# Attention with a relative position bias, then a bilinear feed-forward layer: the band factor made by one-hot products on TensorE, and the first four feed-forward steps interleaved with the last attention pair of batch 0

## The chip, the cores and the metric

The kernel runs on one core of a Trainium2 chip. The metric is the time of one execution on the device in microseconds (us); lower is better. The engines are called as in the profile: PE (TensorE matmuls, with PEld for its weight loads), DVE (VectorE), ACT (ScalarE), POOL (GpSimd) and SP (SyncE, which here only issues transfers).

## What is computed

Inputs are q, k, v of 8 batches, 8 heads, 576 positions and 64 channels, a bias table of 32 buckets by 8 heads, and three weight matrices. The attention output, its heads side by side, is the x of the feed-forward layer.

```python
scores = scale * np.matmul(q, k.transpose(0, 1, 3, 2))      # scale = 1/8
n = np.abs(pos[:, None] - pos[None, :])
bucket = ...            # n itself below 16, then logarithmic, 31 at most
scores = scores + bias_table[bucket].transpose(2, 0, 1)[None]
attn = np.exp(scores - max) / sum
x = matmul(attn, v)     # (8*576, 512), heads side by side
out = ((x @ w_a) * (x @ w_b)) @ w_out        # d_ff = 1536
```

From a distance of 129 on, all positions are in the last bucket. So the kernel multiplies exp(score) by exp(bias - last bias) only in a band around the diagonal; the factor of the last bucket cancels in the softmax.

## The kernel before

**Pairs.** Attention goes by 32 pairs of heads: pair p is batch p // 4, heads 2hp and 2hp + 1 with hp = p % 4. `emit_scores(p, i)` makes the transposed scores of key tile i (128 keys) for both heads into one slot of a ring of two PSUM slots (tag "st"), and ACT takes their exp (L269). `emit_scores_rest` does the last 64 keys and queries (L277, L285, exps L280 and L287). `emit_mult` multiplies the band by the band factor `E_sb` (L303; L298 for the last key tile in batch 0; from pair 4 on the copy `Et_sb`). `emit_av` multiplies by v with a column of ones (L320 for the last 64 keys of both heads, L323 for the others), DVE divides (L331, L333) into `xg`, and `emit_x` transposes that into `xn` (for batch 0 on PE with a copy on DVE, L348 and L349; later by a DMA).

**Band factor.** `emit_table` loads the table (L169), its last row (L170) and a one-hot matrix (L172), subtracts on DVE, takes the exp on ACT, multiplies by the one-hot matrix on PE (L179) to get, for each head, a row of 512 factors by distance, and stores it 32 times over to DRAM (L182). Twelve loads on SP (L188) read it back with a step of 511, one column further for each partition, as `E_sb` (128 x 8 heads x 384), first for heads 0 and 1, then 2 and 3, then 4 to 7; four more (L195) fill `Et_sb`.

**Loads.** All other inputs come by POOL's queue in the program's order: q and k of batch 0 in three parts, v, the first halves of w_a and w_b (`load_w_in(0)`), half of batch 1's q and k, the second halves, the rest of batch 1, w_out. PE transposes q and k for pairs 0 to 9 (`emit_transposes_first`, `emit_transposes`), and ACT or DVE copies them out of PSUM.

**Order.** The order on each engine is that of the program (a manual schedule). In pairs 0 to 3 no feed-forward work can run, as x of batch 0 isn't there yet; matmuls on zeros (`emit_warm`, L403) stand between pair 0's scores. Then come `emit_x(2)`, av of pair 3, `emit_x(3)`, and `QUANTA_FIRST` = 4 feed-forward quanta. A quantum is four matmuls of 512 columns: w_a or w_b (L361, L369) for one slice of 128 of the 1536 channels, with a copy on ACT (L365) or a product on DVE (L372) after it; or a third of an output tile (L378). From pair 4 on each pair has nine steps, and quanta are put between them so that the 36 of the first 512 rows are done by step 47, and one a step from then on.

**Banks.** Four more PSUM banks are used in turn: m0 and m1 for "av" (av, x, table and warm-up), m2 and m3 for "ffn" (quanta, and q/k transposes of batch 0). After pair 3, "av" has m0 alone and "ffn" the other three.

Of the kernel before, what the change touches and what calls it, by code (L numbers as in the profile page):

```python
# [13 lines left out]
def kernel(  # L14
# [11 lines left out]
    nc = tc.nc  # L26
# [42 lines left out]
    assert (bucket_of(np.arange(129, S)) == NB - 1).all()  # L69
    yy = np.arange(512)  # L70
    oh_np = np.zeros((NB, 512), dtype=np.float32)
    oh_np[bucket_of(np.abs(255 - yy)), yy] = 1.0
    oh_handle = nc.inline_tensor(oh_np.astype(ml_dtypes.bfloat16), name="oh_const")
# [83 lines left out]
    oh_sb = const.tile([NB, 512], BF16, name="oh_sb")  # L157
    bt_sb = const.tile([NB, H], FP32, name="bt_sb")
    bl_sb = const.tile([NB, H], FP32, name="bl_sb")
    bd_sb = const.tile([NB, H], FP32, name="bd_sb")  # L160
    eb_sb = const.tile([NB, H, 16], BF16, name="eb_sb")
    tab_sb = const.tile([128, 512], BF16, name="tab_sb")

    tab_dram = nc.dram_tensor("tab_scratch", [H, 32, 512], BF16, kind="Internal")
# [3 lines left out]
    def emit_table():  # L168
        nc.sync.dma_start(out=bt_sb[:, :], in_=bias_table)  # L169
        nc.sync.dma_start(out=bl_sb[:, :],  # L170
                          in_=bias_table[NB - 1:NB, :].to_broadcast([NB, H]))
        nc.sync.dma_start(out=oh_sb[:, :], in_=oh_handle.ap())  # L172
        nc.vector.tensor_tensor(out=bd_sb[:, :], in0=bt_sb[:, :], in1=bl_sb[:, :], op=SUB)

        nc.scalar.activation(
            out=eb_sb[:, :, :],
            in_=bd_sb[:, :].rearrange("b (h a) -> b h a", a=1).to_broadcast([NB, H, 16]), func=ACTF.Exp)
        tp = bank("av", [128, 512], FP32, "tab_ps")
        nc.tensor.matmul(out=tp[:, :], lhsT=eb_sb[:, :, :].rearrange("b h a -> b (h a)"), rhs=oh_sb[:, :],  # L179
                         start=True, stop=True)  # L180
        nc.vector.tensor_copy(out=tab_sb[:, :], in_=tp[:, :])
        nc.sync.dma_start(  # L182
            out=tab_dram.ap().rearrange("h (r a) c -> (h r) a c", a=2),
            in_=tab_sb[:, :].rearrange("p (a c) -> p a c", a=1).to_broadcast([128, 2, 512]))

        for h0, h1 in ((0, 2), (2, 4), (4, H)):
            for r0 in range(0, 128, 32):
# [199 lines left out]
    def all_quanta():  # L387
        for c in range(NCH):
            yield from ffn_quanta(c)

    quanta = all_quanta()


# [48 lines left out]
    for p in range(4):  # L442
# [26 lines left out]
        if p == 0:  # L469
            emit_warm(2)  # L470
# [119 lines left out]
```

## Time and profile before

| | |
|---|---|
| three runs | 418.82, 419.52, 420.39 us (median 419.52) |
| profiled execution | 419.12 us |
| its span | 417.4 us, granted clock 0.998 |
| PE busy | 402.5 us (96%) |
| DVE, ACT, POOL busy | 233.9, 231.2, 79.0 us |
| bytes moved | 47.71 MB, 11.75 MB of them in the first 70 us |
| first quantum on PE | 35.09 us |
| first scores of pair 4 | 39.22 us |

The span goes from the first instruction to the last; the execution has 1.7 us more around it. A matmul's busy time includes its way through the array, and successive matmuls overlap, so PE's share is an upper bound. In a group of instructions or a timeline, a row gives the engine, the line, the operation, what is written from what, and in brackets how long the engine had been idle and what released it.

### The profile page before, as it was taken

The page shows a single profiled execution, that of the slowest core. Times are in us where ns is not written, and L with a number is a line of the kernel's source. Part 1 is how long each engine was busy: PE and PEld are TensorE (multiplying, and loading weights), DVE is VectorE, ACT ScalarE, POOL GpSimd, SP SyncE. Part 2 cuts the span into 40 slices and gives each one's busy share as a digit, 9 for nine tenths or more (in the row PEclk, how much of TensorE's full clock was granted, in tenths as well). Part 3 has the DMA queues.
Part 4 walks back from the last instruction along what each step waited for, and adds up shares of the span by engine and source line. Part 5 has one row for each costly group of instructions (what it writes and reads, how often), then busy time and mean ns, then how long its engine had stood idle before and what let it go on. Part 6 is the DMA issues. An engine that isn't in the chain of part 4 may idle for free.

```text
span 417.4 us, 8452 instructions
## 1 busy us (share of the span) xinstructions
PE 402.5 (96%) x3346; PEld 206.4 (49%) x3404; DVE 233.9 (56%) x568; ACT 231.2 (55%) x313; POOL 79.0 (19%) x136
## 2 busy tenths in 40 slices
PE   8789899999999999999999999999999999999996
PEld 2455355555455455454555555454554554444442
DVE  3486666676555755575556656665556553332331
ACT  4984788566755665476646674567556631321320
POOL 8744641113111311103011311130000000000000
PEclk9999999999999999999999999999999999999999
DMA  9999999699759686978697977983342012002002
GB/s 111 183 209 206 166 189 105 135 208 158 107 94 207 114 100 104 213 102 112 102 178 136 134 103 151 177 127 52 71 121 45 17 40 93 2 0 101 2 0 101
DMA packets 111176, 47.71 MB, mean 114 GB/s; under 512 B 85120, under 2 KB 106528, under 8 KB 111136
## 3 DMA queue, kind: packets, MB, share of 16 engines
q0 software_dynamic: 54304, 18.88, 42.2%
q1 hardware_dynamic: 56832, 28.29, 28.0%
q8 instruction: 26, 0.43, 0.4%
q14 instruction: 14, 0.11, 0.1%
HBM read 38.77 MB, written 16.19 MB: 132 GB/s over the span
## 4 chain that ended last, share of the span: by engine, by line
PE 85%; DMA 8%; POOL 3%; issue 2%; DVE 1%; ACT 1%; POOLq 0%; DVEq 0%
PE po L378 23%; PE pb L369 21%; PE pa L361 21%; PE av L323 8%; PE st L267 7%; DMA wb<-in_moe_w_b_dram 6%; PE av L320 2%; DMA vb<-in_v_dram 2%; PE st L285 2%; PE st L277 1%; POOL vb L129 1%; POOL kl L108 0%; PE tr L219 0%; POOL ql L108 0%; ACT at L269 0%
## 5 line engine op out<-in xcount | busy, mean ns | idle before, releaser
L269 ACT ACTIVATE at<-st 128x1024 bf16<-128x1024 f32 x128 | 124.0, 1022 | 52.1 <-PE st L267 51.2
L372 DVE TENSOR_TENSOR g<-pb,ha 128x512 bf16<-128x512 f32 x108 | 74.6, 691 | 77.0 <-PE pb L369 54.0
L365 ACT ACTIVATE ha<-pa 128x512 f32<-128x512 f32 x108 | 64.7, 599 | 92.2 <-PE pa L361 91.0
L369 PE MATMUL pb<-xn,wb 128*128 128x512 bf16 x407 | 109.0, 379 | 1.5
L361 PE MATMUL pa<-xn,wa 128*128 128x512 bf16 x417 | 108.8, 379 | 0.5
L378 PE MATMUL po<-wo,g 128*128 128x512 bf16 x415 | 99.7, 379 | 0.8
L303 DVE TENSOR_TENSOR at<-at,E 128x768 bf16<-128x768 bf16 (+2 forms) x128 | 61.5, 501 | 7.9 <-DMA E<-tab_scratch 4.1
L323 PE MATMUL av<-vb,at 128*128 128x65 bf16 x1280 | 64.7, 194 | 0.3 <-DVE at L303 0.2
L378 PEld LDWEIGHTS <-g 128*128 128x128 bf16 x432 | 39.6, 98 | 49.1 <-issue 7.9
L323 PEld LDWEIGHTS <-at 128*128 128x128 bf16 x1280 | 55.4, 98 | 16.5 <-issue 1.2
L369 PEld LDWEIGHTS <-wb 128*128 128x128 bf16 x432 | 38.7, 97 | 46.4 <-issue 8.0
L361 PEld LDWEIGHTS <-wa 128*128 128x128 bf16 x432 | 38.4, 97 | 43.2 <-issue 7.0
L382 DVE COPY ob<-po 128x512 f32<-128x512 f32 x36 | 24.9, 691 | 53.9 <-PE po L378 53.9
L267 PE MATMUL st<-qkT 64*128 64x512 bf16 x256 | 40.8, 385 | 2.6 <-ACT at L280 0.9
L320 PE MATMUL av<-vb,at 128*128 128x130 bf16 x160 | 35.4, 221 | 2.5 <-DVE xn L349 1.2
L496 POOL COPY pace<-at 1x1 bf16<-1x1 bf16 x22 | 4.2, 193 | 173.0 <-DVE at L303 172.9
L333 DVE TENSOR_TENSOR xg<-av,rc 128x384 bf16<-128x384 f32 x64 | 31.4, 491 | 2.2
L129 POOL DMA_DIRECT2D vb<-in_v_dram x36 | 30.7, 864 | 7.9 <-PE pb L369 2.2
L280 ACT ACTIVATE at<-st 128x512 bf16<-128x512 f32 x32 | 19.1, 597 | 23.0 <-PE st L277 23.0
L331 DVE RECIPROCAL rc<-av 128x6 f32<-128x6 f32 x64 | 11.8, 184 | 27.6 <-PE av L323 27.6
L320 PEld LDWEIGHTS <-at 128*128 128x128 bf16 x160 | 15.6, 98 | 17.1 <-issue 1.6
L287 ACT ACTIVATE at<-st 128x576 bf16<-128x576 f32 x32 | 20.7, 646 | 0.0
(51 smaller groups left out, 177.8 us busy)
## 6 DMA issues: line engine op xcount, KB each, us to landing
out_dram<-ob SPq DMA_DIRECT2D x36, 256.0 KB, 2.3
qk_scratch<-qkn SPq DMA_DIRECT2D x22, 288.0 KB, 4.5
ql<-in_q_dram POOLq DMA_DIRECT2D x15, 288.0 KB, 5.7
kl<-in_k_dram POOLq DMA_DIRECT2D x15, 288.0 KB, 6.9
vb<-in_v_dram POOLq DMA_DIRECT2D x28, 128.0 KB, 6.7
wa<-in_moe_w_a_dram POOLq DMA_DIRECT2D x4, 384.0 KB, 13.9
wb<-in_moe_w_b_dram POOLq DMA_DIRECT2D x4, 384.0 KB, 13.6
wo<-in_moe_w_out_dram POOLq DMA_DIRECT2D x4, 384.0 KB, 7.9
```

Source lines behind the costliest of these rows:

```text
L129: nc.gpsimd.dma_start(out=vb2[b % 2][:, h0:h1, i, 0:Dh], in_=v[b, h0:h1, 128 * i:128 * i + 128, :].transpose([1, 0, 2]))
L267: nc.tensor.matmul(out=st[:, hh, :], lhsT=kT[r, 128 * i:128 * i + 128], rhs=qT[r, 0:512], start=True, stop=True)
L269: nc.scalar.activation(out=at[:, 2 * i:2 * i + 2, 0:512], in_=st[:, :, :], func=ACTF.Exp, scale=scale)
L303: nc.vector.tensor_tensor(out=at[:, sl, q0:q0 + w], in0=at[:, sl, q0:q0 + w], in1=e, op=MULT)
L320: nc.tensor.matmul(out=pav[:, j, :, :], lhsT=at[:, 8, 128 * jq:128 * jq + 128], rhs=vb[:, 2 * hp:2 * hp + 2, 4, :], start=True, stop=False)
L323: nc.tensor.matmul(out=pav[:, j, hh, :], lhsT=at[:, 2 * i + hh, 128 * jq:128 * jq + 128], rhs=vb[:, 2 * hp + hh, i, :], start=False, stop= ...
L333: nc.vector.tensor_tensor(out=xo.rearrange("p j (h d) -> p j h d", h=2), in0=pav[:, :, :, 0:Dh], in1=rc[:, 0:n, :, :].to_broadcast([128, n ...
L361: nc.tensor.matmul(out=ps[:, :], lhsT=wa_sb[:, mc, 128 * df:128 * df + 128], rhs=xn[:, mc, 512 * c:512 * c + 512], start=(mc == 0), stop=( ...
L365: nc.scalar.activation(out=ha[:, :], in_=ps[:, :], func=ACTF.Copy)
L369: nc.tensor.matmul(out=ps[:, :], lhsT=wb_sb[:, mc, 128 * df:128 * df + 128], rhs=xn[:, mc, 512 * c:512 * c + 512], start=(mc == 0), stop=( ...
L372: nc.vector.tensor_tensor(out=g[:, df, :], in0=ps[:, :], in1=ha[:, :], op=MULT)
L378: nc.tensor.matmul(out=ps[:, :], lhsT=g[:, df, 128 * tt:128 * tt + 128], rhs=wo_sb[:, df, :], start=(df == 0), stop=(df == NDF - 1))
```

## The change

The band factor is no longer read from DRAM. Four one-hot matrices, one above the other (32 rows each, shifted by one position each), and a mask are one constant of 128 x 544. The table stands four times in 128 partitions. A product of 128 one-hot columns with the 128 x 32 right side (four blocks on the diagonal, one for each shift) gives four columns of the band for 8 heads; 16 such products fill a bank, and DVE copies it to 64 columns of `E_sb`, heads first. Six bands (`emit_band(0)` to `emit_band(5)`) stand in pair 0 in the places of warm-up matmuls (eleven go, the first six and the last two stay). `Et_sb` is copied from `E_sb` on POOL. The DVE memsets of `set_k` and `set_at` move ahead of the table. The loads from `load_w_in(1)` on stand behind pair 0's `emit_scores_rest`, with the copy of `Et_sb` among them.

The first four quanta become `EarlyQuanta`: two of their accumulators in one slot of the "st" ring, two in the "ffn" banks; each `part(mc)` runs the four matmuls of one head pair's rows of x, and parts stand before and after pair 3's av and `emit_x(3)`. `emit_x(2)` copies on ACT. Two more quanta come before pair 4, `QUANTA_FIRST` is 6.

```diff
     yy = np.arange(512)
-    oh_np = np.zeros((NB, 512), dtype=np.float32)
-    oh_np[bucket_of(np.abs(255 - yy)), yy] = 1.0
-    oh_handle = nc.inline_tensor(oh_np.astype(ml_dtypes.bfloat16), name="oh_const")
+    oh_np = np.zeros((4, NB, 544), dtype=np.float32)
+    for g in range(4):
+        oh_np[g, bucket_of(np.abs(252 - yy + g)), yy] = 1.0
+        oh_np[g, :, 512 + 8 * g:520 + 8 * g] = 1.0
+    oh_handle = nc.inline_tensor(oh_np.reshape(4 * NB, 544).astype(ml_dtypes.bfloat16), name="oh_const")
     ident = const.tile([128, 128], BF16, name="ident")
...
-    oh_sb = const.tile([NB, 512], BF16, name="oh_sb")
-    bt_sb = const.tile([NB, H], FP32, name="bt_sb")
-    bl_sb = const.tile([NB, H], FP32, name="bl_sb")
-    bd_sb = const.tile([NB, H], FP32, name="bd_sb")
-    eb_sb = const.tile([NB, H, 16], BF16, name="eb_sb")
-    tab_sb = const.tile([128, 512], BF16, name="tab_sb")
-    tab_dram = nc.dram_tensor("tab_scratch", [H, 32, 512], BF16, kind="Internal")
+    oh_sb = const.tile([128, 544], BF16, name="oh_sb")
+    bt_sb = const.tile([128, H], FP32, name="bt_sb")
+    bl_sb = const.tile([128, H], FP32, name="bl_sb")
+    eb_sb = const.tile([128, H], FP32, name="eb_sb")
+    ebd_sb = const.tile([128, 4, H], BF16, name="ebd_sb")
     E_sb = wpool.tile([128, H, 384], BF16, name="E")
     Et_sb = wpool.tile([128, H // 2, 192], BF16, name="Et")
     def emit_table():
-        nc.sync.dma_start(out=bt_sb[:, :], in_=bias_table)
+        for g in range(4):
+            nc.sync.dma_start(out=bt_sb[32 * g:32 * g + 32, :], in_=bias_table)
         nc.sync.dma_start(out=bl_sb[:, :],
-                          in_=bias_table[NB - 1:NB, :].to_broadcast([NB, H]))
+                          in_=bias_table[NB - 1:NB, :].to_broadcast([128, H]))
         nc.sync.dma_start(out=oh_sb[:, :], in_=oh_handle.ap())
-        nc.vector.tensor_tensor(out=bd_sb[:, :], in0=bt_sb[:, :], in1=bl_sb[:, :], op=SUB)
-        nc.scalar.activation(
-            out=eb_sb[:, :, :],
-            in_=bd_sb[:, :].rearrange("b (h a) -> b h a", a=1).to_broadcast([NB, H, 16]), func=ACTF.Exp)
-        tp = bank("av", [128, 512], FP32, "tab_ps")
-        nc.tensor.matmul(out=tp[:, :], lhsT=eb_sb[:, :, :].rearrange("b h a -> b (h a)"), rhs=oh_sb[:, :],
-                         start=True, stop=True)
-        nc.vector.tensor_copy(out=tab_sb[:, :], in_=tp[:, :])
-        nc.sync.dma_start(
-            out=tab_dram.ap().rearrange("h (r a) c -> (h r) a c", a=2),
-            in_=tab_sb[:, :].rearrange("p (a c) -> p a c", a=1).to_broadcast([128, 2, 512]))
-        for h0, h1 in ((0, 2), (2, 4), (4, H)):
-            for r0 in range(0, 128, 32):
-                nc.sync.dma_start(
-                    out=E_sb[r0:r0 + 32, h0:h1, :],
-                    in_=bass.AP(tensor=tab_dram, offset=16384 * h0 + 127 - r0,
-                                ap=[[511, 32], [16384, h1 - h0], [1, 384]]))
+        nc.vector.tensor_tensor(out=bt_sb[:, :], in0=bt_sb[:, :], in1=bl_sb[:, :], op=SUB)
+        nc.scalar.activation(out=eb_sb[:, :], in_=bt_sb[:, :], func=ACTF.Exp)
+        nc.vector.tensor_tensor(
+            out=ebd_sb[:, :, :],
+            in0=eb_sb[:, :].rearrange("b (a h) -> b a h", a=1).to_broadcast([128, 4, H]),
+            in1=oh_sb[:, 512:544].rearrange("b (a h) -> b a h", a=4), op=MULT)
+    def emit_band(k):
+        ps = bank("av", [128, 64, H], FP32, f"E{k}")
+        for j in range(16):
+            s = 380 - 4 * (16 * k + j)
+            nc.tensor.matmul(out=ps[:, 4 * j:4 * j + 4, :], lhsT=oh_sb[:, s:s + 128],
+                             rhs=ebd_sb[:, :, :], start=True, stop=True)
+        nc.vector.tensor_copy(out=E_sb[:, :, 64 * k:64 * k + 64],
+                              in_=ps[:, :, :].rearrange("p c h -> p h c"))
+    def copy_band_tail():
         for hh in range(2):
-            for r0 in (0, 32):
-                nc.sync.dma_start(
-                    out=Et_sb[64 * hh + r0:64 * hh + r0 + 32, :, :],
-                    in_=bass.AP(tensor=tab_dram, offset=16384 * hh + 127 - r0,
-                                ap=[[511, 32], [32768, 4], [1, 192]]))
+            r, c0 = slice(64 * hh, 64 * hh + 64), 64 * hh
+            nc.gpsimd.tensor_copy(out=Et_sb[r, :, :], in_=E_sb[r, hh::2, c0:c0 + 192])
...
-    def emit_x(p):
+    def emit_x(p, act=False):
...
         ps = bank("av", [128, 5, 128], BF16, f"xT{p}")
         for jq in range(5):
             nc.tensor.transpose(ps[:, jq, :], xg_of[p][:, jq, :], ident[:, :])
-        nc.vector.tensor_copy(out=xn[:, hp, S * b:S * b + S],
-                              in_=ps[:, :, :].rearrange("p j t -> p (j t)")[:, 0:S])
+        o, i = xn[:, hp, S * b:S * b + S], ps[:, :, :].rearrange("p j t -> p (j t)")[:, 0:S]
+        if act:
+            nc.scalar.activation(out=o, in_=i, func=ACTF.Copy)
+        else:
+            nc.vector.tensor_copy(out=o, in_=i)
     def ffn_bank(name):
         return bank("ffn", [128, 512], FP32, name)
-    def ffn_quanta(c):
-        g = wrk.tile([128, NDF, 512], BF16, tag="g", name=f"g{c}")
-        for df in range(NDF):
+    class EarlyQuanta:
+        def __init__(self):
+            self.g = wrk.tile([128, NDF, 512], BF16, tag="g", name="g0")
+            ring = pst.tile([128, 2, 512], FP32, tag="st", name="pab0_0")
+            self.ps = [(ring[:, 0, :], ring[:, 1, :]),
+                       tuple(ffn_bank(f"{n}0_1")[:, :] for n in ("pa", "pb"))]
+        def part(self, mc):
+            for df in range(2):
+                for ps, w_sb in zip(self.ps[df], (wa_sb, wb_sb)):
+                    nc.tensor.matmul(out=ps, lhsT=w_sb[:, mc, 128 * df:128 * df + 128],
+                                     rhs=xn[:, mc, 0:512], start=(mc == 0), stop=(mc == NMC - 1))
+                if mc == NMC - 1:
+                    ha = wrk.tile([128, 512], FP32, tag="ha", name=f"ha0_{df}")
+                    nc.scalar.activation(out=ha[:, :], in_=self.ps[df][0], func=ACTF.Copy)
+                    nc.vector.tensor_tensor(out=self.g[:, df, :], in0=self.ps[df][1], in1=ha[:, :],
+                                            op=MULT)
+    def ffn_quanta(c, early=None):
+        g = early.g if early else wrk.tile([128, NDF, 512], BF16, tag="g", name=f"g{c}")
+        for df in range(2 if early else 0, NDF):
             ps = ffn_bank(f"pa{c}_{df}")
             for mc in range(NMC):
                 nc.tensor.matmul(out=ps[:, :], lhsT=wa_sb[:, mc, 128 * df:128 * df + 128],
...
                     nc.sync.dma_start(out=out[r0:r0 + 128, :], in_=ob[:, :])
                 yield
-    def all_quanta():
+    def all_quanta(early):
         for c in range(NCH):
-            yield from ffn_quanta(c)
-    quanta = all_quanta()
+            yield from ffn_quanta(c, early if c == 0 else None)
     warm = const.tile([128, 512], BF16, name="warm")
...
             nc.tensor.matmul(out=wp[:, :], lhsT=warm[:, 0:128], rhs=warm[:, :], start=True, stop=True)
-    QUANTA_FIRST = 4
+    QUANTA_FIRST = 6
     emit_warm(6)
     qk_alloc(0)
     qk_alloc(1)
+    set_k(0)
+    set_k(1)
+    set_at(0)
+    set_at(1)
     emit_table()
-    set_k(0)
     load_qk(0, 0, 2)
     make_identity(nc, ident)
     load_qk(0, 2, 4)
...
     load_v(0, 4, 8)
     load_w_in(0)
     load_qk(1, 0, 4)
-    load_w_in(1)
-    set_v(1, nc.gpsimd)
-    load_qk(1, 4, H)
-    load_v(1, 0, H)
-    load_v_tail(1)
-    load_w_out()
     emit_transposes_first(0)
-    emit_warm(3)
-    set_k(1)
-    set_at(0)
-    set_at(1)
+    emit_band(0)
     emit_tails(0)
     def emit_avs(p, g0, g1):
...
                 emit_x(p - 2)
                 emit_avs(p - 1, 0, 4)
         else:
-            emit_warm(3)
+            emit_band(1)
+            emit_band(2)
         emit_scores(p, 2)
         if p:
             emit_avs(p - 1, 0 if p == 1 else 4, 4 if p == 1 else 6)
         else:
-            emit_warm(3)
+            emit_band(3)
+            emit_band(4)
         emit_scores(p, 3)
         if p < 3:
             emit_transposes_first(p + 1, k_act=(p == 1))
         if p:
             emit_avs(p - 1, 4 if p == 1 else 6, 10)
         else:
-            emit_warm(2)
+            emit_band(5)
             emit_mult(0, 0)
             emit_mult(0, 1)
         emit_mult(p, 2)
         emit_scores_rest(p)
         if p == 0:
             emit_warm(2)
+            load_w_in(1)
+            set_v(1, nc.gpsimd)
+            load_qk(1, 4, H)
+            copy_band_tail()
+            load_v(1, 0, H)
+            load_v_tail(1)
+            load_w_out()
         emit_mult(p, 3)
         emit_mult(p, 4)
         if p < 3:
             emit_tails(p + 1)
-    emit_x(2)
+    emit_x(2, act=True)
+    early = EarlyQuanta()
+    early.part(0)
     emit_avs(3, 0, 10)
+    early.part(1)
     emit_x(3)
+    early.part(2)
+    early.part(3)
+    quanta = all_quanta(early)
     banks.update(av=(0,), ffn=(2, 3, 1))
-    next(quanta)
-    next(quanta)
     emit_transposes_first(4, ring=True)
     emit_tails(4)
     relayout_qk(1, 2, 4)
-    for _ in range(QUANTA_FIRST - 2):
+    for _ in range(QUANTA_FIRST - 4):
         next(quanta)
```

## The prediction

> **What bounds it now.** I read first the busy time by stretches (columns: stretch, its length, then busy us and instruction count of PE, PEld, DVE, ACT, POOL, then granted clock, DMA share, GB/s).
>
> ```profile
> 0.00:10.00 10.00, 8.20 (x43) 2.61 (x43) 3.59 (x10) 3.79 (x5) 8.56 (x22) 1.00 0.91 110
> 10.00:20.00 10.00, 8.26 (x123) 4.84 (x125) 4.23 (x12) 9.28 (x13) 7.80 (x12) 1.00 1.43 178
> 20.00:30.00 10.00, 7.72 (x131) 5.30 (x131) 9.07 (x29) 9.18 (x13) 4.66 (x11) 1.00 1.18 209
> ...
> 40.00:50.00 10.00, 8.70 (x61) 3.89 (x60) 6.15 (x14) 9.20 (x13) 5.12 (x8) 1.00 1.69 162
> 50.00:60.00 10.00, 9.76 (x113) 5.67 (x113) 7.21 (x18) 7.49 (x11) 6.13 (x10) 1.00 1.27 201
> ```
>
> From 50 us PE works without a gap to speak of; what is saved before that is saved at the end. Between 10 and 32 us ACT is the full engine (exps of pairs 0 to 3), and DMA stands near 205 GB/s until 40 us. ACT's timeline shows how closely it runs, and where PE holds it up:
>
> ```profile
> 8.45 4.01 ACT L269 ACTIVATE at<-st 128x1024 bf16<-128x1024 f32 x4 [2.45 <-PE st L267]
> ...
> 17.07 1.02 ACT L269 ACTIVATE at<-st 128x1024 bf16<-128x1024 f32 x1 [0.24 <-PE st L267]
> ...
> 19.60 0.60 ACT L280 ACTIVATE at<-st 128x512 bf16<-128x512 f32 x1 [0.42 <-PE st L277]
> ...
> 25.86 0.60 ACT L280 ACTIVATE at<-st 128x512 bf16<-128x512 f32 x1 [0.82 <-PE st L277]
> ...
> 31.49 0.65 ACT L287 ACTIVATE at<-st 128x576 bf16<-128x576 f32 x1
> ```
>
> ACT waits 0.24 + 0.42 + 0.82 + 0.24 = 1.72 us in pairs 1 to 3 (the last stands at 30.99). Behind these stand, in DVE's timeline, three waits for the band factor's transfers, and on PE one for V:
>
> ```profile
> 14.92 1.76 DVE L303 TENSOR_TENSOR at<-at,E 128x512 bf16<-128x512 bf16 x4 [2.10 <-DMA E<-tab_scratch]
> ...
> 19.09 0.89 DVE L303 TENSOR_TENSOR at<-at,E 128x512 bf16<-128x512 bf16 x2 [1.55 <-DMA E<-tab_scratch]
> ...
> 23.44 0.89 DVE L303 TENSOR_TENSOR at<-at,E 128x512 bf16<-128x512 bf16 x2 [0.49 <-DMA E<-tab_scratch]
> ```
> ```profile
> 49.75 0.22 PE L320 MATMUL av<-vb,at 128*128 128x130 bf16 x1 [0.67 <-DMA vb<-in_v_dram]
> ```
>
> The chain of waits runs through the same load (start, length): V of batch 1 is the last link of a queue of loads.
>
> ```profile
> 14.91 12.76 DMA wb<-in_moe_w_b_dram
> ...
> 27.96 13.92 DMA wb<-in_moe_w_b_dram
> ...
> 42.42 7.20 DMA vb<-in_v_dram
> ```
>
> **Start of the scores: -0.1 us (-0.35 to +0.9).** The memsets moved ahead of the table on DVE (0.17 + 0.17 + 1.15 us from 1.14) end at 2.65, before any bias load lands: free. SP issues 0.46 us apart; bl_sb becomes its fifth load and the one-hot table its sixth, at 3.05 instead of 1.67, four times as large. It landed in 2.3 us; E's 48 KB pieces took 2.5 to 5.6 us beside other loads. So 5.4 to 7.5, I take 6. The small product of eb_sb and the mask waits for it on DVE, and queued behind that is pair 0's k copy (6.52), which the first scores await. At 6 nothing is late. Band 0 replaces three warm-up matmuls (0.43 us apart from 6.41), so scores could start at 7.45 instead of 7.80; I take 7.7.
>
> **Bands in pair 0: +1.0 us (0 to +1.8).** Eleven warm-up matmuls go, 96 products of 32 columns come, and six PSUM copies on DVE at 0.69 us (the 128x512 cast of tab_sb, 690 ns). No row has such a product. The av groups start nine matmuls (650 columns, 128-column weights) in 0.31 us, 34 ns each; transposes start every 26 ns (0.31 us for 12), and 40 ns early on (0.50 us for 12). Hence 16 products take 0.55 us plus 0.2 until the last is out, and 0.65 to 1.1 plus 0.2 while PE is slow. With S the scores' start, bands 1 and 2 run from S+1.0 to S+2.6, and scores(0,2) stand behind them in PE's order: the third exp starts at S+3.25 instead of S+2.65, 0.6 late. Band 4 takes band 2's bank and waits for its copy (DVE S+2.8 to S+3.5): S+3.7 to S+4.3; scores(0,3) queue behind, fourth exp at S+4.95, 0.7 later again. That is 1.3; PE was at full speed by 9.9, in the middle of this, so 1.0. The low end is PE gaps that hold everything, the high end a PE slow throughout. Band 5's copy ends at 14.5, so the multiplications start 0.4 before the 14.92 above; the band factor is hardly earlier for pair 0.
>
> **Waits in pairs 1 to 3: -1.3 us (-1.7 to -0.6).** The 1.55 and 0.49 us on DVE have nothing left to wait for. DVE is full from 19.9 to 30, so starting some 1.5 us ahead lets xn and q/k copies come in time for PE, and ACT's 1.72 us of waits mostly close. Not all: mult and copies still follow the exps.
>
> The last exp of pair 3 thus ends at 32.14 - 0.4 = 31.75.
>
> **End of the front and the early quanta: +0.35 - 1.26 us.** Before, av(3) starts at 32.18 and ends at 33.9, xT(3) waits for xg until 34.75, the quanta run to 36.8, scores(4) start at 39.22 with four quanta done. After: part 0 (four matmuls, 0.865 us) once st's slot is free at 31.35, av(3) 32.2 to 33.9, part 1 to 34.75 over DVE's reciprocal and product, xT(3) 0.27, part 2 to 35.9 over the xn copy (0.46), part 3 to 36.75, transposes 0.63, two quanta 1.73: scores(4) at 39.15 to 39.2. So 31.75 has become 39.2, 0.35 given back, with two quanta more. x(2)'s copy moves to ACT (0.65), which has nothing queued until ha at 36. Two quanta fewer are then due by step 47, by the rate 30/47 for 32/47: one less in pair 4, one in pair 7. In pair 7 PE is full: 0.86. Pair 4 is ACT's (8.18 of 8.29 us, busy nearly throughout from 39.65 to 47.35); only the rest's 0.21 wait and the order of the last two quanta are gained, 0.4. If the cover of ACT were gone it would be 0.86 too.
>
> **Transfers and POOL: -0.7 us (-0.8 to 0) and +0.2 (0 to +1.5).** Gone are the 256 KB store, 12 E and 4 Et loads (0.79 + 0.20 MB) on SP; 1.24 MB at 205 GB/s is 6 us, by the queue's engine time 4. V of batch 1 would land at 44 to 45.6 instead of 49.62, wanted at 48.3: PE's 0.67 goes. On POOL the moved loads keep their order; they wait behind the two Et copies, which wait for band 5 (14.5), when POOL, held by its earlier loads, is nowhere near (28.7 for the memsets before). The copies move 64x768 each: by the memset (0.32 for 260 elements) 0.95, by the select (0.29 for 128) 1.74. In 1.9 to 3.5 us no load is issued, while each has 12 to 14 us to landing: covered by the backlog; without it V would be that late, still before 48.3. On DVE, a pair of L303 took 1.10 instead of 0.89 beside POOL's memsets at 28.36; over 3 us that is 0.5, in DVE's fullest stretch, half hidden. High end: both copies block once each.
>
> The Trainium skill (SBUF — State Buffer, Who interferes with whom) goes further: a GpSimd instruction that reads SBUF and a DVE product with two SBUF inputs exclude each other for the whole instruction. By that the +0.2 would stand near its upper end; no row here shows a POOL read of this size.
>
> **Sum.** -0.1 + 1.0 - 1.3 + 0.35 - 1.26 - 0.7 + 0.2 = -1.8 us. The profiled execution took 419.12 us (span 417.4, 1.7 around it), so 417.3; it lies 0.4 below the median of the three runs, 419.52, and in the median's terms I say **417.7 us**.
>
> **Rivals.** First, *bands cost nothing*: 34 ns products fit into PE's idle time (1.7 to 2.3 us per 10) and scores start at 7.45. Then -1.8 - 1.0 - 0.25 = -3.05: 416.5. Against it: the wait for a bank's copy.
>
> Second, *V still sets the time*: loads are issued against a backlog, and if the relief does not reach V, av(4) starts at 49.75 as now. The front's gain is swallowed; one quantum more is done by then: -0.86, 418.7. For it: POOL's copies stand just before V. Against: 205 GB/s is flat, so bytes removed are time.
>
> Third, the other side, *PE stays slow*. Same warm-up matmul, same granted clock of 1.00, two speeds:
>
> ```profile
> 8.77 1.23 PE L403 MATMUL warm<-warm 128*128 128x512 bf16 x3
> ...
> 10.25 0.82 PE L403 MATMUL warm<-warm 128*128 128x512 bf16 x3
> ```
>
> The early ones start 0.43 us apart, the later 0.215. The change takes the dense matmuls that stand before the switch. If bands don't do their work, pair 0 gives +3.3 (bands 1.0 each, transposes 1.1, rest 0.9) and pair 1 needs 4 x 0.43 scores, 0.9 rest, 5 x 0.54 av and 1.0 transposes, 6.3 us on PE with some 1.2 of handovers, 7.5 against 6.7: +0.8. Recovered waits shrink to 0.9: -0.1 + 3.3 + 0.8 - 0.9 + 0.35 - 1.26 - 0.7 + 0.2 = +1.7, 421.2. It decides once the switch comes later than some 20 us; at 13 to 16 us it costs about 1 and leaves 418.7.
>
> The Trainium skill (TensorE: Matmul & The Clock Gate, Part 1) has PE at half rate until a window of about 3.4 us was busy; it adds that small matmuls start no closer than some 25 ns, so that a 32-column product leaves the array idle about half the time. By it the gate opens later and the sum nears the third rival's.
>
> **Numbers.** Likeliest 0.46 (own range 416.6 to 418.9), bands free 0.21, V late 0.15, PE slow 0.18. 0.5% (2.1 us, about what can be told from no change) puts the faster line at 417.4: 0.4 of the likeliest's chance and all of the first rival's lie below, 0.40; slower 0.18; the rest 0.42. Range 415.4 to 420.9.
>
> **What will tell.** ACT's first exps: gaps of 0.6 before the third and the fourth; the first L303 near 14.5 with no DMA wait; last exp of pair 3 near 31.8; scores(4) near 39.2; no wait for vb near 48; in PE's timeline the spacing of the band products, and the time when 512-column scores shorten from 0.63 to 0.38 us. I am wrong if the one-hot table lands after 7.5, or if that switch comes after pair 0.

## The result, and the profile after

| | before | after |
|---|---|---|
| median (lowest to highest), 22 runs each | 419.35 us (418.24 to 422.86) | 421.21 us (420.64 to 422.21) |
| ratio | | 1.0034, interval 1.0020 to 1.0049 |
| profiled execution, its span | 419.12, 417.4 us | 421.17, 419.4 us |
| first scores of pair 0 | 7.80 us | 9.18 us |
| end of the last exp of pair 3 | 32.14 us | 32.75 us |
| first scores of pair 4 (quanta done) | 39.22 us (4) | 40.24 us (6) |
| first scores of pair 9 | 85.38 us | 86.14 us |
| start of DVE's last copy | 413.73 us | 415.35 us |

The change made the kernel slower by a third of a per cent, where a gain of 1.8 us was forecast. The busy time by stretches of the changed kernel, in the columns of the prediction:

```profile
0.00:10.00 10.00, 5.53 (x50) 2.45 (x50) 3.52 (x10) 2.20 (x4) 8.57 (x22) 1.00 0.89 96
10.00:20.00 10.00, 9.17 (x201) 6.56 (x199) 8.37 (x21) 9.73 (x13) 8.39 (x13) 1.00 1.35 151
20.00:30.00 10.00, 7.79 (x130) 5.20 (x129) 9.19 (x24) 10.00 (x14) 7.53 (x15) 1.00 1.20 207
...
40.00:50.00 10.00, 8.63 (x57) 3.81 (x56) 4.88 (x12) 8.29 (x11) 4.46 (x7) 1.00 1.60 189
50.00:60.00 10.00, 9.09 (x96) 4.96 (x95) 6.44 (x18) 7.29 (x11) 2.72 (x5) 1.00 1.24 154
```

ACT has 2.20 us of work in the first ten instead of 3.79: the scores come late. From 10 to 30 us it has only 0.27 us of gap left, which is what the change was expected to bring. But from 50 to 60 us PE has 9.09 us instead of 9.76, so the stretch in which it was full now has gaps.

ACT's timeline (start, length, operation, in brackets the idle time before it and what ended it):

```profile
9.83 2.96 ACT L268 ACTIVATE at<-st 128x1024 bf16<-128x1024 f32 x3 [2.28 <-PE st L266]
13.06 1.02 ACT L268 ACTIVATE at<-st 128x1024 bf16<-128x1024 f32 x1 [0.27 <-PE st L266]
...
15.59 3.77 ACT L268 ACTIVATE at<-st 128x1024 bf16<-128x1024 f32 x4
...
31.61 0.60 ACT L279 ACTIVATE at<-st 128x512 bf16<-128x512 f32 x1 [1.04 <-PE st L276]
32.10 0.65 ACT L286 ACTIVATE at<-st 128x576 bf16<-128x576 f32 x1
```

The first exps are 1.38 us later than before. In pair 0 there is one wait of 0.27 us (0.6 and 0.7 were expected), and none from 15.59 until pair 3, where the wait is 1.04 us (0.24 before).

The start is read from DVE's timeline:

```profile
6.60 0.17 DVE L175 TENSOR_TENSOR bt_sb<-bt_sb,bl_sb 128x8 f32<-128x8 f32 x1 [3.96 <-DMA bl_sb<-in_bias_table_dram]
8.26 0.19 DVE L177 TENSOR_TENSOR ebd_sb<-eb_sb,oh_sb 128x32 bf16<-128x32 f32 x1 [1.49 <-DMA oh_sb<-oh_const]
8.37 0.75 DVE L249 COPY qkT<-tr 128x576 bf16<-128x576 bf16 x1
```

The one-hot table, issued at 3.06, landed at 8.2, and the k copy behind its product is what the first scores await at 9.18. In the six other traces with these loads it landed at 7.6 to 7.8, and the scores started at 8.62 to 8.82, once at 9.65. PE from there:

```profile
9.18 1.04 PE L266 MATMUL st<-qkT 64*128 64x512 bf16 x4
10.15 1.04 PE L187 MATMUL E<-ebd_sb,oh_sb 128*128 128x32 bf16 x32
11.12 0.61 PE L266 MATMUL st<-qkT 64*128 64x512 bf16 x2
11.66 1.03 PE L187 MATMUL E<-ebd_sb,oh_sb 128*128 128x32 bf16 x32
12.62 0.39 PE L266 MATMUL st<-qkT 64*128 64x512 bf16 x2
```

A pair of scores takes 0.61 us at 11.12 and 0.39 at 12.62: PE comes to its full speed in between. Two bands take 0.97 us, less than an exp (1.02), so ACT hardly waits.

Pair 3's wait has its cause one engine further. DVE, and below it POOL:

```profile
27.55 0.95 DVE L255 COPY bd<-qkT 64x128 bf16<-64x128 bf16 x2
28.54 1.54 DVE L302 TENSOR_TENSOR at<-at,E 128x512 bf16<-128x512 bf16 x2
```
```profile
27.64 1.70 POOL L197 COPY Et<-E 64x768 bf16<-64x768 bf16 x2
```

The same pairs of instructions earlier in this trace:

```profile
17.38 0.39 DVE L255 COPY bd<-qkT 64x128 bf16<-64x128 bf16 x2
17.80 0.89 DVE L302 TENSOR_TENSOR at<-at,E 128x512 bf16<-128x512 bf16 x2
```

While POOL copies Et, DVE takes 0.95 us for two small copies and 1.54 for two products, instead of 0.39 and 0.89: 1.2 us more. Taken singly, one DVE instruction is longer beside each of POOL's copies: a small copy takes 0.75 us instead of 0.19 and ends at 28.51, as POOL's first copy does at 28.45; a product takes 1.07 instead of 0.43.

Steps of the span, before against after, each difference taken between two marks of the traces:

| step | predicted | measured |
|---|---|---|
| start of the scores (7.80, 9.18) | -0.1 | +1.38 |
| bands in pair 0 (scores to the first exp of pair 1: 13.97, 15.59) | +1.0 | +0.24 |
| waits of pairs 1 and 2 (to the first exp of pair 3: 26.94, 26.75) | -1.3, with pair 3 | -1.81 |
| pair 3 and POOL's copies (to 32.14, 32.75) | +0.2 | +0.80 |
| end of the front (to 39.22, 40.24) | +0.35 | +0.41 |
| pairs 4 to 8 (46.16, 45.90 us) | -1.26 - 0.7 | -0.26 |
| pair 9 to the last copy | none | +0.86 |
| last copy to the end of the span (3.62, 4.02) | none | +0.40 |
| sum | -1.8 | +2.0 |

The steps of the front are taken from single executions, and the front differs between executions of the same code. The old band code stands unchanged in two of the experiments, early_only and before_rate30, the new one in all others and in the changed kernel itself.

- The first scores start at 6.75 to 7.80 us in the three traces with the old code, and at 8.62 to 9.65 in the seven with the new one and its loads on SP.
- From the first exp of pair 1 to that of pair 3 it is 12.97, 13.95 and 15.74 us with the old code, and 11.16 in eight of the eleven traces with the new one. So -1.81 is the smallest of three gains. In the two longer ones PE's granted clock falls to 0.50 in this stretch (15 to 22 us in before_rate30, 20 to 22 in early_only).

Pairs 4 to 8 hold the largest miss, and they are steadier. Their lengths, from first scores to first scores, with the quanta done when pair 5 starts:

| kernel | pair 4 | 5 | 6 | 7 | 8 | quanta |
|---|---|---|---|---|---|---|
| before | 8.29 | 10.13 | 9.22 | 9.42 | 9.10 | 10 |
| after | 8.28 | 10.27 | 9.80 | 8.41 | 9.14 | 11 |
| bands_only | 8.28 | 9.30 | 9.22 | 9.42 | 9.10 | 10 |
| before_rate30 | 8.29 | 10.26 | 9.81 | 8.41 | 9.14 | 9 |
| all_fixed_skip4 | 7.83 | 9.30 | 9.22 | 9.42 | 9.10 | 10 |

The quantum less in pair 7 brings its 1.01 us. The one in pair 4 brings nothing. Pair 5 gets no shorter although V is there in time, and pair 6 becomes 0.58 us longer with as many quanta as before.

At the end of the loop the changed kernel has a wait that the one before had not. PE:

```profile
346.87 5.34 PE L400 MATMUL po<-wo,g 128*128 128x512 bf16 x24
352.99 1.02 PE L383 MATMUL pa<-xn,wa 128*128 128x512 bf16 x4 [0.78 <-DVE ob L404]
```

### The profile page after: what moved, and what is told of

It is laid out like the page before. It is cut to its first block, busy times and chain, and to the rows that moved or that the text cites. A ratio compares the mean times of both kernels' runs of the same rounds, so it can differ in the third digit from the quotient of the medians.

```text
span 419.4 us, 8666 instructions
## 1 busy us (share of the span) xinstructions
PE 403.6 (96%) x3488; PEld 208.0 (50%) x3488; DVE 236.0 (56%) x573; ACT 231.3 (55%) x314; POOL 80.6 (19%) x138
## 4 chain that ended last, share of the span: by engine, by line
PE 90%; ACT 4%; DVE 3%; DMA 1%; issue 1%; SPq 0%; DVEq 0%
PE po L400 23%; PE pb L391 22%; PE pa L383 22%; PE av L322 9%; PE st L266 7%; PE av L319 2%; ACT at L268 2%; PE st L284 2%; PE st L276 1%; DMA oh_sb<-oh_const 1%; DVE at L302 1%; PE tr L218 1%; DVE xg L332 0%; PE E L187 0%; PE pab L370 0%
## 5 line engine op out<-in xcount | busy, mean ns | idle before, releaser
L394 DVE TENSOR_TENSOR g<-pb,ha 128x512 bf16<-128x512 f32 x106 | 73.2, 691 | 83.1 <-PE pb L391 60.2
L387 ACT ACTIVATE ha<-pa 128x512 f32<-128x512 f32 x106 | 63.4, 598 | 92.3 <-PE pa L383 92.3
L400 PE MATMUL po<-wo,g 128*128 128x512 bf16 x432 | 101.3, 380 | 0.0
L391 PEld LDWEIGHTS <-wb 128*128 128x128 bf16 x424 | 37.7, 97 | 47.2 <-issue 10.2
```

The lines of the kernel that those rows point to most:

```text
L387: nc.scalar.activation(out=ha[:, :], in_=ps[:, :], func=ACTF.Copy)
L391: nc.tensor.matmul(out=ps[:, :], lhsT=wb_sb[:, mc, 128 * df:128 * df + 128], rhs=xn[:, mc, 512 * c:512 * c + 512], start=(mc == 0), stop=( ...
L394: nc.vector.tensor_tensor(out=g[:, df, :], in0=ps[:, :], in1=ha[:, :], op=MULT)
L400: nc.tensor.matmul(out=ps[:, :], lhsT=g[:, df, 128 * tt:128 * tt + 128], rhs=wo_sb[:, df, :], start=(df == 0), stop=(df == NDF - 1))
```

## The experiments

They ran in three groups of four, each group beside runs of the kernel before on one chip (its medians: 419.48 of 26 runs, 420.01 of 29, 419.71 of 30). Ratios are to these, with their 95% interval. The changed kernel's 421.21 us stands beside another 419.35, so it is best compared by ratio.

### The two halves of the change alone

**bands_only**: the changed kernel with the first four quanta, `emit_x(2)` and `QUANTA_FIRST` as before.

```diff
-    emit_x(2, act=True)
-    early = EarlyQuanta()
-    early.part(0)
+    emit_x(2)
     emit_avs(3, 0, 10)
-    early.part(1)
     emit_x(3)
...
-    QUANTA_FIRST = 6
+    QUANTA_FIRST = 4
```

> The changed kernel with the four quanta of the kernel before in their old places (x(2) copied on DVE again), so that the band part stands alone. Theory A (the loss is a late one-hot table, POOL's copy of Et_sb, a loop that two quanta fewer leave idle, and a bank that the last quanta find taken): the front loses 0.5 to 0.8 us against the kernel before (scores start 1.4 late, waits of pairs 1 and 2 recovered, the copy costs 0.8), the loop has its 32 quanta back and no wait for V, no bank stall: 419.2 to 420.0 us, 0 to +0.6 on the kernel before. Theory B (the early quanta are worth the 0.9 us that the prediction priced, and the bands cost all the loss): 422.1 us. Theory C (TensorE stays slow after the bands): above 421, with 512-column scores at 0.61 us after pair 0.

Measured: 419.20 us, 0.9990 (0.9975 to 1.0004). By itself the new band factor is worth nothing that can be told from no change, though V's wait is gone with it: pair 5 takes 9.30 us instead of 10.13. It loses in front (scores(4) at 39.97 instead of 39.22) what it gains there. The front of the kernel before is not always that early: before_rate30, which has the same front, reached pair 4 at 40.50.

**early_only**: the kernel before with the early quanta, the ACT copy of x(2) and six quanta before pair 4.

> The kernel before with only the early quanta, x(2) on ACT and the 30/47 rate. Theory A: front with two quanta more costs 0.35 to 0.4 us, the loop gives back only some 0.3 of the 1.73 us, the last quanta find their bank taken (0.8): 420.0 to 420.6 us, slower than before. Theory B: 418.4 us.

Measured: 421.48 us, 1.0041 (1.0024 to 1.0058). The early quanta are the harmful half, 0.9 us worse than expected. The wait of 0.78 us after the attention is in this trace too, at 353 us. Pair 9 took 12.09 us, in the kernel before and the changed one 11.08, with a wait of PE for x(7), which those two don't have:

```profile
90.36 0.38 PE L384 MATMUL pa<-xn,wa 128*128 128x512 bf16 x1 [0.85 <-DMA xn<-xg]
```

Why x(7) landed later here wasn't followed up.

### Where the quanta stand

**before_rate30**: the kernel before, with 30 quanta in 47 steps instead of 32; nothing is done earlier in exchange.

```diff
-            if n >= 47 or (n + 1) * (36 - QUANTA_FIRST) // 47 > n * (36 - QUANTA_FIRST) // 47:
+            if n >= 47 or (n + 1) * 30 // 47 > n * 30 // 47:
```

> The kernel before with nothing changed but the rate, 30 quanta in 47 steps (so 34 are done by then). Theory A (the same steps as in the changed kernel leave PE idle): pairs 4 to 8 take 45.8 to 46.2 us as with 32, and two quanta remain for the end: 420.6 to 421.2 us. If the loop is bound by PE, pairs 4 to 8 shorten by 1.7 us and the time stays at 419.4 us.

Measured: 421.44 us, 1.0029 (1.0012 to 1.0046). Two quanta fewer from pair 4 to 8 shorten these pairs by 0.25 us (46.16 to 45.91), not by 1.7, and the pairs have the changed kernel's lengths to 0.01 us (the table above). So the loss in pairs 5 and 6 comes from the steps in which quanta fall. PE has no wait for V in pair 5 of this trace, and pair 5 is as long as in the changed kernel.

How, pair 5 shows. DVE of the changed kernel, then of bands_only:

```profile
53.20 0.69 DVE L394 TENSOR_TENSOR g<-pb,ha 128x512 bf16<-128x512 f32 x1 [1.50 <-PE pb L391]
53.81 0.61 DVE L120 COPY qkn<-ql 96x768 bf16<-96x768 bf16 x2
```
```profile
51.15 0.69 DVE L394 TENSOR_TENSOR g<-pb,ha 128x512 bf16<-128x512 f32 x1
51.75 0.62 DVE L120 COPY qkn<-ql 96x768 bf16<-96x768 bf16 x2
```

and PE's transposes that need these copies, again in the changed kernel and in bands_only:

```profile
52.05 1.04 PE L391 MATMUL pb<-xn,wb 128*128 128x512 bf16 x4
...
54.21 0.96 PE L218 MATMUL tr<-ident,qkn 96*128 96x96 bf16 x12 [0.81 <-DVE qkn L120]
```
```profile
52.11 1.02 PE L383 MATMUL pa<-xn,wa 128*128 128x512 bf16 x4
...
52.97 0.68 PE L218 MATMUL tr<-ident,qkn 96*128 96x96 bf16 x12
```

Two things differ. With an odd number of quanta done, w_a and w_b slices have changed places; and a quantum now falls in the pair's fourth step and none in the fifth, where it was the other way round. So the quantum just ahead of the transposes is a w_b slice (PE at 52.05), whose product is on DVE; it stands in DVE's order ahead of the copies, and these ahead of the transposes. In bands_only the w_b slice comes earlier, and the quantum before the transposes is a w_a slice, which ACT copies and which PE works on while DVE copies. From the start of the pair to the transposes it is 5.69 us against 4.72, the whole loss of pair 5. No run parts the odd count from the changed steps, and how pair 6 loses its 0.58 us wasn't followed.

**rate32**: the changed kernel with 32 quanta in 47 steps in place of 30, so that the steps are those of the kernel before.

> The changed kernel with the loop's rate of the kernel before, 32 quanta in 47 steps for 30, so that the two early quanta stay ahead until the end. Theory A (with 30 PE is idle in pairs 4 to 8): PE's idle time between 41 and 86 us goes down by 1 to 1.7 us and the time with it: 419.5 to 420.2 us. Rival (the loop is bound by PE and the two quanta are only moved): 421.2 us, less than 0.3 of change.

Measured: 424.33 us, 1.0104 (1.0084 to 1.0124); neither theory had that. Pairs 5 and 6 took 9.31 and 9.22 us again, and the five together 45.49, with two quanta more than in the changed kernel. But the quanta of the first 512 rows are now done two steps early, the next ones need x(7), and x(7) is late. PE, then DVE:

```profile
91.03 0.38 PE L383 MATMUL pa<-xn,wa 128*128 128x512 bf16 x1 [4.15 <-DMA xn<-xg]
```
```profile
87.20 0.62 DVE L120 COPY qkn<-ql 96x768 bf16<-96x768 bf16 x2 [4.57 <-DMA qk_scratch<-qkn]
```

**after_hold**: the same steps, but only 30 quanta, so that none falls in the last three.

```diff
+            if n >= 47 or min(30, (n + 1) * 32 // 47) > min(30, n * 32 // 47):
```

> The changed kernel with its six early quanta and 30 in the loop, but these 30 at the steps of the 32/47 rate, and none in the last three steps before 47. Theory A (what costs is where the quanta fall: at the 30/47 steps pairs 5 and 6 take 1.5 us longer with the same number of quanta): pairs 5 and 6 take 9.2 to 9.4 us each instead of 10.27 and 9.80, pair 9 starts 0.5 to 0.9 earlier; the quanta of the next 512 rows then come up to 1.7 us sooner, until they wait for x of pair 7: 418.8 to 420.7 us. Rival (six ahead and 30 left is too few whatever the steps): pair 9 starts where it did, 421 us or more.

Measured: 424.41 us, 1.0104 (1.0079 to 1.0128); missed by 4. Pairs 5 and 6 took 9.31 and 9.22 us as expected, pair 9 started 0.47 earlier than in the changed kernel, and then DVE stood still for 5.08 us. SP's issues, then DVE:

```profile
78.18 0.34 SPq L406 DMA_DIRECT2D out_dram<-ob  x1
78.57 2.26 SPq L127 DMA_DIRECT2D qk_scratch<-qkn  x2
```
```profile
87.87 0.62 DVE L120 COPY qkn<-ql 96x768 bf16<-96x768 bf16 x2 [5.08 <-DMA qk_scratch<-qkn]
```

The buffer that the stores of q and k leave comes free late, DVE waits for it, and behind DVE's copy stands the division that x(7) needs. An output tile, done earlier, was stored 0.39 us ahead of q and k here; in the kernel before and the changed one it was 1.85 and 2.35 us, and DVE waited 1.39 and 1.31. In all_fixed_skip4, where it is 1.87 us again, DVE waits 1.90. That this store is the cause is read from the order of issue and wasn't tried by itself. In any case, with the other steps as they are, doing these quanta earlier costs more than the steps of the changed kernel do.

### The start of the scores

**table_two_queues**: the four small table loads go to ACT's queue, the last row and the one-hot table are SP's first, and the difference has a tile of its own. The edit of the queue (the others are left out here):

```diff
-            nc.sync.dma_start(out=bt_sb[32 * g:32 * g + 32, :], in_=bias_table)
+            nc.scalar.dma_start(out=bt_sb[32 * g:32 * g + 32, :], in_=bias_table)
```

> The changed kernel; the four bias loads are issued from ACT's queue while SP issues bl_sb and the one-hot table first and second, and the difference has a tile of its own. Theory A: the table lands before 5.5 us instead of 8.1, first scores near 7.4 instead of 9.18, and as ACT has no idle time between 20 and 30 us, pair 4's scores move by 1.2 to 1.7 and the time to 419.5 to 420.0 us. Theory C: the scores start earlier, but the gate opens no earlier and the time moves by less than 0.4 us.

Measured: 419.16 us, 0.9988 (0.9972 to 1.0005), the whole loss against before made good. DVE and PE:

```profile
5.94 0.19 DVE L178 TENSOR_TENSOR ebd_sb<-eb_sb,oh_sb 128x32 bf16<-128x32 f32 x1 [0.28 <-ACT eb_sb L177]
```
```profile
7.54 1.04 PE L267 MATMUL st<-qkT 64*128 64x512 bf16 x4 [0.32 <-DVE qkT L250]
...
11.02 0.61 PE L267 MATMUL st<-qkT 64*128 64x512 bf16 x2
```

Scores start at 7.54 instead of 9.18, and pair 4 at 38.63 instead of 40.24. That 1.64 us at the start is 1.61 there is not the start alone: pair 3 is 0.80 shorter, as POOL's copies start at 28.10 and no longer fall on the same work of DVE, and pairs 0 to 2 are 0.83 longer. Of these, 0.58 stands in pair 1, where PE now waits for the third part of k:

```profile
17.79 0.45 PE L238 MATMUL tr<-ident,kl 96*64 96x96 bf16 x12 [0.70 <-DMA kl<-in_k_dram]
```

The other 0.25 is in pair 0. PE is still slow at 11.02 (a pair of these scores takes 0.61 us; at full speed 0.39). From the first scores to the first exp of pair 1 it is 6.41 us in the four traces with the new code where the fourth pair of scores took 0.39, and 6.66 to 7.05 in five of the six where it took 0.60; the sixth is all_fixed, where the first scores ran at full speed. Queue, order of the loads and the tile were changed together, so what each of them is worth isn't known.

**warm_in_gap**: four warm-up matmuls in PE's gap before band 0.

```diff
     emit_transposes_first(0)
+    emit_warm(4)
     emit_band(0)
```

> The changed kernel with four warm-up matmuls ahead of band 0, in PE's idle time before the one-hot table lands (6.2 to 8.2 us), so that the gate opens earlier. Theory A (the bands don't care for the gate, 29 to 32 ns each in either state): the second 512-column scores become 0.39 us long instead of 0.61, and the time stays within 0.4 us of 421.2. Theory C: 419.5 to 420.3 us.

Measured: 420.80 us, 1.0025 (1.0008 to 1.0041). It says little. k landed at 6.74 us instead of 5.50, and the warm-up matmuls, behind its transposes, held PE past the landing of the table (7.68):

```profile
7.40 1.89 PE L423 MATMUL warm<-warm 128*128 128x512 bf16 x4
```

Scores started at 9.65, and the pair of scores at 11.58 still took 0.61 us, so PE was not at full speed sooner. What a PE at full speed through all bands would bring wasn't measured. In all_fixed PE came to the bands at full speed, but did not keep it: its first pair of scores took 0.39 us, the second 0.54, the third 0.61.

```profile
7.35 0.77 PE L267 MATMUL st<-qkT 64*128 64x512 bf16 x4 [0.36 <-DVE qkT L250]
...
9.02 0.61 PE L267 MATMUL st<-qkT 64*128 64x512 bf16 x2
```

### POOL's copies and the banks

**copy_late**: `copy_band_tail()` moved behind the loads of batch 1's V.

```diff
-            copy_band_tail()
             load_v(1, 0, H)
             load_v_tail(1)
+            copy_band_tail()
```

> The changed kernel with POOL's two copies of Et_sb behind the loads of batch 1's V instead of ahead of them. Theory A (the copies hold up DVE in pair 3, and through the copy of xn and PE's av the last exps by 0.8 us): two products on DVE near 28.5 us take 0.9 again instead of 1.54, scores of pair 4 start 0.6 to 0.9 earlier; as the loop is no shorter, 420.3 to 420.7 us. Rival (POOL and DVE share nothing, and the 1.54 is a wait of another kind): no change in pair 3, 421.2 us.

Measured: 420.26 us, 1.0000 (0.9982 to 1.0017). POOL copies at 38.52. DVE's small copies and the two products in question:

```profile
27.19 0.39 DVE L255 COPY bd<-qkT 64x128 bf16<-64x128 bf16 x2
27.62 0.43 DVE L302 TENSOR_TENSOR at<-at,E 128x512 bf16<-128x512 bf16 x1
28.37 0.56 DVE L302 TENSOR_TENSOR at<-at,E 128x768 bf16<-128x768 bf16 x1 [0.33 <-ACT at L268]
```

From the first scores to pair 4 the time is 30.26 us (8.82 to 39.08) instead of 31.06: the 0.80 of the table.

**bank_turn**: two turns are skipped when "ffn" gets its four banks.

```diff
     banks["ffn"] = (0, 1, 2, 3)
+    turn["ffn"] += 2
```

> The changed kernel with the turn of the feed-forward banks moved on by two where the four-bank stage begins. If the last output tile's bank is what the next product waits for (0.78 us on PE behind DVE's copy at 352 us), that wait is gone and the time is 420.3 to 420.5 us. If that wait only uncovers another, 421.2 us.

Measured: 419.83 us, 0.9984 (0.9964 to 1.0005). PE:

```profile
346.75 5.34 PE L400 MATMUL po<-wo,g 128*128 128x512 bf16 x24
351.92 1.03 PE L383 MATMUL pa<-xn,wa 128*128 128x512 bf16 x4
```

The wait is gone. The early quanta take two turns of the ffn banks instead of four, so the count stands at 202 and not at 204 when the attention ends, and the first slice after it falls on the bank that the last output tile has just filled: it must wait for DVE to copy it. The profiled executions differ by 1.1 us (421.17, 420.06), the wait by 0.78; the ratios differ by 0.5%, 2.1 us, with intervals of ±0.2% and ±0.15%, so the size is taken from the trace: the wait of 0.78 is gone, and from pair 9 to the last copy it is 328.27 us, 0.94 less than in the changed kernel and as in the kernel before (328.35).

### What is left when these are mended

**bands_fixed**: bands_only with the table on two queues and the late copy. **all_fixed**: the changed kernel with the table on two queues, the late copy and the bank turn. **all_fixed_skip4**: all_fixed, with 30 quanta in the steps of the kernel before, two of pair 4's left out:

```diff
+            if n >= 47 or n not in (4, 5) and (n + 1) * 32 // 47 > n * 32 // 47:
```

> The band part alone (four quanta in their old places), with the table's loads on two queues and POOL's copy behind V's loads. Theory A: scores start near 7.5 (8.71 in the band part alone, 1.2 earlier) and pair 3 loses nothing to POOL (0.8 to 0.9): against the band part alone -1.6 to -2.1, 417.0 to 417.7 us, 0.4 to 0.6% faster than the kernel before. If these gains are taken back by V or ACT, 418.3 us or more.

> The changed kernel with three repairs: table loads on two queues, POOL's copy behind V's loads, the bank's turn. The single repairs gave 1.3 to 2.0, 0.9 and 0.8 to 1.4 us; if they add up, 417.0 to 418.0 us. Against the band part with two of the repairs, theory A (the early quanta bring nothing) says within 0.7 us of it; if the early quanta are worth what was priced, 0.9 below it.

> The same with the 30 quanta of the loop at the steps of the 32/47 rate, two of them left out in pair 4 (steps 4 and 5), so that all later quanta and the stores of the output stand where they stood in the kernel before. Theory A (where quanta fall decides): pair 4 takes 7.3 to 7.8 us instead of 8.28, pairs 5 and 6 9.2 to 9.4 instead of 10.27 and 9.80, and x of pair 7 comes as much earlier: 415.3 to 416.5 us. If pair 4 is ACT's whatever PE has to do, 8.2 us for it and 416.3 to 417.2 us.

Measured: bands_fixed 417.51 us, 0.9953 (0.9937 to 0.9970); all_fixed 418.29, 0.9965 (0.9951 to 0.9979), a little above what was expected; all_fixed_skip4 417.42, 0.9950 (0.9930 to 0.9971), not the 415.3 to 416.5 of the first theory but 0.2 above the second's range. The second's reason, pair 4 at 8.2 us, did not come: pair 4 took 7.83, close to the first's 7.3 to 7.8, and pairs 5 and 6 took 9.30 and 9.22 as the first had it. What the first left out is pair 7, which has its sixth quantum back and takes 9.42 us instead of 8.41; so the five pairs are 1.04 us shorter than in all_fixed. Bands without early quanta are as good as anything with them. The mends don't add up: with the early table alone pair 3 already had its 0.80 us back, so the late copy has nothing left to give there. In all_fixed_skip4 pair 4 with two quanta fewer is 0.45 us shorter than in bands_only, not 1.7: PE waits for ACT there.

```profile
42.89 0.38 PE L277 MATMUL st<-bd,qkT 128*128 128x128 bf16 x4 [0.53 <-ACT at L269]
43.81 0.41 PE L285 MATMUL st<-qkT,bd 128*128 128x288 bf16 x2 [0.53 <-ACT at L269]
```

Pair 9 starts at 82.91 us, against 83.06 in bands_fixed, but the scores of pair 0 started 0.14 earlier too. From the last exp of pair 3 to pair 4 it is 7.49 us in all ten traces with early quanta and 7.09 in the four without. So two quanta done in front cost 0.40 there, and 0.45 comes back: 0.05 us is left, and the medians (417.42 and 417.51) show no difference.

## Why the prediction was wrong

**The early quanta: the step that failed most.** "Two quanta fewer are then due by step 47, by the rate 30/47 for 32/47: one less in pair 4, one in pair 7." The count is right, and pair 7 gave 1.01 us where 0.86 was said. But the rate moves the other quanta as well, and these were not looked at. Pairs 5 and 6 keep their six, in other steps, and lose 0.97 and 0.58 us against bands_only. before_rate30 shows the same lengths with nothing but the rate changed, and rate32, after_hold and all_fixed_skip4 have the short ones back. Pair 4's 0.4 is nothing at 30/47; all_fixed_skip4 found 0.45, for two quanta. (ACT is busy for 7.48 us of that pair's 8.29, not 8.18.) That the work itself was worth 0.86 a quantum was the deeper error: a quantum taken out of pairs 4 to 8 leaves a gap wherever another engine sets the pair, as ACT does pair 4. Against 0.40 us more in front, the early quanta had nothing to give.

**V's load.** "PE's 0.67 goes": it does, as bands_only shows (pair 5 shorter by 0.83). In the changed kernel the loss by the steps takes its place, which is why pair 5 looks unchanged. The second rival, that V still sets the time, is refuted.

**The start.** "So 5.4 to 7.5, I take 6. … At 6 nothing is late." The bound came from E's pieces, issued later and to other tiles, and it was too low: 8.2. The prediction's own sign of being wrong, a landing after 7.5, came true. The text named the consequence, but gave it no price beyond 0.9; it cost 1.38, and with the loads of table_two_queues (landing at 4.4) the scores start at 7.54. The table's last row, now for 128 partitions instead of 32, was slow as well: it landed after 3.9 us (1.7 before). That didn't decide here, as its exp was done at 7.0, ahead of the one-hot table.

**Bands in pair 0.** +1.0 was too much, +0.24 came. While PE was slow, 32 products kept it 0.97 us (10.15 until the next matmul at 11.12), 30 ns each; at full speed the last 16 took 0.41 us (13.58 to 13.99), 26 ns each. The bounds had 0.65 to 1.1 us for 16 while slow. The Trainium skill (TensorE: Matmul & The Clock Gate, Part 1) gives a floor of some 25 ns for such products at full speed, near the 26; that a slow PE adds so little no row before could tell. It is not always +0.24: where PE stays slow longer, pair 0 takes up to 7.05 us (bands_only) against 6.17 in the kernel before, +0.88, still inside the stated 0 to +1.8. Waits of pairs 1 and 2 closed wholly, -1.81 against this trace of the kernel before.

**POOL.** +0.2 with an upper end of 1.5 became +0.80. The copies took 0.82 us each, a little under the 0.95 to 1.74 taken from POOL's memset and select, but DVE's delay was not "half hidden": it was ACT's next wait. The row that +0.2 rests on was misread: of the 1.10 us at 28.36, the two products take 0.43 and 0.56, as ever, and 0.12 between them is a wait for ACT's exp, so POOL's memsets delayed nothing. What happened is the stated high end, "both copies block once each": 1.2 us on DVE, 0.80 of it on the way to the last exp. Here the rule of the Trainium skill (SBUF — State Buffer, Who interferes with whom) that had been set against the row was the better guide: DVE's two products took 1.54 instead of 0.89 us, and copy_late removed both the overlap and the 0.80.

**The end.** The front's +0.35 was measured at +0.41. Not in the sum at all were the turn of the banks (the whole +0.86, shown by bank_turn) and the last 0.40.

**The rivals.** The third, "PE stays slow", named 421.2 us and the time is 421.21, but that is chance. Its mechanism did not happen: PE is at full speed at 12.6 us, not after 20, pair 0 lost 0.24 us in all instead of 3.3 (0.88 at most in the other traces), pair 1 gained, and table_two_queues, where PE is as slow at 11.0, is faster by 1.9 us by the ratios. (The stated range ended at 420.9 and so left this rival's own time out.) The first, "bands cost nothing", is the closest to what the bands did; its 416.5 failed at the other steps.

## What to carry to other kernels

Work pulled ahead is worth only as much as its engine sets the time of the stage that it leaves; and where engines run in a fixed order, look at where the rest of it lands, since filler work that moves to another step can delay what stands behind it, and a count of turns that shifts by two can put a bank's next use on its last. A table that is built on the chip must land before the first thing queued behind its products: put its loads first, here with a second queue beside, and price small loads by the slowest of the trace. Run each half of a change alone: here one half was neutral with two losses in it that could be mended (0.5% faster without them), and the other had next to nothing to give. And look at the same stage in several traces before a difference in it is given a cause: this front differed by 1.3 us between executions of the same code.

## What the runs showed of the hardware that was not expected

- Small loads at the start were slow and depended on their place: the one-hot table (136 KB) landed after 4.5 to 5.1 us as SP's sixth load (seven traces) and after 3.2 to 3.3 as its second (four); the 32 KB one of the kernel before after 2.3; the 4 KB of the last row after 3.6 to 4.3 as the fifth load and 2.6 to 3.4 as the first.
- In the changed kernel's trace PE came to full speed between 11.3 and 12.6 us, in five others with the bands it was still slow at 11.0 to 12.2; with the old band code it was at full speed by 9.9 at the latest in pair 0. Pair 0 was 0.25 to 0.64 us longer in the traces where it was slow at the fourth scores (all_fixed excepted).
- The granted clock doesn't show every slow stretch. In the changed kernel's trace it reads 1.00 while a pair of scores takes 0.61 us. Where PE had been at full speed and fell back, it reads 0.50: from 8 to 11 us in all_fixed and copy_late and to 14 us in bands_only, while the bands ran, and from 15 to 22 us in before_rate30, after DVE had waited 3.80 us for E.
- From the end of DVE's last copy to the end of the span it is 2.9 to 3.0 us in the three kernels with the old band code and 3.3 to 3.4 us in all eleven with the new one. What makes these 0.4 us wasn't tried.
